# Spectral mixer with a gated MLP: roundings and rests of operands queued apart, two weight loads on GpSimd's queue, 128 spare bytes for 192

## The chip, the cores and the metric

The kernel runs on one core of a Trainium2 chip. The metric is the device time of one execution in microseconds, lower is better. The core has five engines that work through queues of their own and wait for each other by semaphores: TensorE (PE in the profile; its weight loads are PEld), VectorE (DVE), ScalarE (ACT), GpSimd (POOL) and SyncE (SP). In this kernel SyncE only issues DMAs, and GpSimd only DMAs as well, apart from making an identity matrix.

## What is computed

All data is float32: x has 2048 tokens of 512 features.

```python
x = A_x
xn = layernorm(x)
a = einsum("bsd,ed->bse", xn, dft_hid_re)          # 512 x 512
b = einsum("bsd,ed->bse", xn, dft_hid_im)
s = einsum("ts,bse->bte", dft_seq_re, a) - einsum("ts,bse->bte", dft_seq_im, b)   # 2048 x 2048
y = layernorm(xn)
h = gelu(einsum("bsd,df->bsf", y, w1) + b1)        # 512 -> 1792
g = silu(einsum("bsf,fd->bsd", h, w2) + b2)        # 1792 -> 512
return x + s * g
```

## The kernel before

**Two numbers for one.** A float32 product runs on TensorE in the fp32r type. Each operand is split in two: `hi` is the value rounded to fp32r, written by ScalarE (line 64), and `lo` is the rest, `src - hi`, written by VectorE (line 65). A product is three matmuls: hi x hi, hi x lo, lo x hi. So every operand costs one ScalarE instruction and then one VectorE instruction that needs it. `split_into`, `split` and `split_two` issue the two next to each other.

**Seven products for eight.** The larger matrix products are done by Strassen-Winograd steps: sums of quarters of the operands are formed first (`a_sums`, `y_sum`, `w1_sums`), then seven products, then sums of results.

**Stages.** (1) For the first half of the tokens, transposes and the hidden DFT (`dft_mm`, `dft_out`), i = 0 to 7. (2) For the second half the hidden DFT by seven products, `q_product(1)` to `q_product(7)`, in the order 1, 2, 5, 6, 3, 7, 4; each has four column blocks c, and after each block the steps that are listed in the call are queued. (3) The first MLP layer: seven groups j of w1, each with seven products p (`h_product`, line 624), in the order of `h_seq`. Groups 0 and 1 are done for one half of the tokens (tau 1, `ONE`) first, then for the other (tau 0, `ZERO`); groups 2 to 6 for both at once. (4) The second MLP layer (`m_product`). (5) The sequence DFT with the gate and the output. Stages 4 and 5 run their matmuls in `multiply_by` (line 809) and line 1127.

**Order.** The program is scheduled by hand: each engine's queue has its instructions in the order in which the Python code issues them, and an engine whose next instruction waits does nothing else. What stands where in the code is therefore the schedule. Products of stage 2 and 3 take moving or stationary operands called y (from the normalised input, tau 0 and 1, in the versions 11, 21, 22, t1, t2, t3, t4), A (from the DFT weights) and w1.

**Around the change.** `y_centre` and `y_scale` apply mean and scale to the transposed input; `y_sum` forms t1 to t4 in place. `w1_load` (SyncE, line 425) fetches a group's weights into the one buffer of the pool `wr`, so it waits until the rest of the group before has read it; `w1_sums` forms four sums; `w1_split` rounds and rests all seven operands (128 x 1792). In stage 3, product p of a group goes to one of three accumulators (y for 1, 6, 7, 4; z for 5, 3; x for 2). `h_after` copies the accumulator after 1, 5 and 6 on ScalarE (line 640), adds it on VectorE after 2, 3 and 7 (lines 669, 675, 679) with a gelu behind it (line 629), and takes a gelu straight from it after 4. Since 1, 6, 7 and 4 share one accumulator, product 6 waits for the copy after 1, product 7 for the copy after 6, and product 4 for the addition after 7. Product 4 of a group stands in the sequence behind product 5 of the next group. `y_late` lists what is issued just before a product of the groups 0 and 1 in their first half.

**Memory.** The pool `op` (39 tiles of 4,096 bytes a partition) holds operands and guests; behind it lie the constants, among them a tile `spare` that nothing uses (line 105), then `small`, and then the pools that change with the stages (`lpa`, `fp`; later `wr`, `wp` with the w1 operands, `lpm`; later `lp`, `gp`). In each partition the compiled kernel has `op` from byte 16,512, the constants from 176,256, and `wr` and `wp` from 180,416 and 188,608.

Of the kernel before, what the change touches and what calls it, by code (L numbers as in the profile page):

```python
# [8 lines left out]
F32 = mybir.dt.float32  # L9
F32R = mybir.dt.float32r  # L10
BF16 = mybir.dt.bfloat16
I32 = mybir.dt.int32
AF = mybir.ActivationFunctionType
ALU = mybir.AluOpType

P = 128
W = 512
# [5 lines left out]
def fnet_mixer_kernel(ctx: ExitStack, tc: tile.TileContext, x, xT, ct, wt, w1, w2, b1, b2, out):  # L23
    nc = tc.nc
# [11 lines left out]
    consts = ctx.enter_context(tc.tile_pool(name="consts", bufs=1))  # L36
# [9 lines left out]
    def operand(name):  # L46
        return op.tile([P, 2, W], F32R, tag="op", name=name)
# [15 lines left out]
    def split_into(hi, lo, src):  # L63
        nc.scalar.activation(hi, src, AF.Copy)  # L64
        nc.vector.tensor_sub(lo, src, hi.bitcast(F32))  # L65
# [6 lines left out]
    def split_two(src, name):  # L72
        hi, lo = operand(name + "h"), operand(name + "l")
        split_into(hi, lo, src)
        return hi, lo

    def both(row):
        return row[:, None, :].broadcast_to([P, 2, W])

# [22 lines left out]
    sq = consts.tile([P, NC], F32, name="sq")  # L102


    consts.tile([P, 3 * W // 32], F32, name="spare")


    def stats(mv, t, i):
# [101 lines left out]
    room_w = {}  # L210
# [203 lines left out]
    def xt_prepare(b):  # L414
        for k in range(NK // 2):
            xt_centre(b, k)
        for k in range(NK // 2):
            xt_make(b, k)


    w1_raw, w1_op = {}, {}

    def w1_load(j):
        w1_raw[j] = wr.tile([P, 8, 2 * P], F32, tag="w", name=f"w1r{j}")
        nc.sync.dma_start(out=w1_raw[j][:, 4:, :], in_=w1[j])

    def w1_sums(j):
        s1, s2, s3, s4, a11, a12, a22, a21 = (w1_raw[j][:, q, :] for q in range(8))
# [2 lines left out]
        nc.vector.tensor_sub(s2, s1, a11)  # L431
        nc.vector.tensor_sub(s4, a12, s2)

    def w1_split(j):
        hi, lo = (wp.tile([P, 7, 2 * P], F32R, tag="w", name=f"w1{v}{j}") for v in "hl")
        split_into(hi, lo, w1_raw[j][:, :7, :])
        w1_op[j] = (hi, lo)

    y_raw, y_op = {}, {}

    def y_centre(b, k2):
        nc.vector.tensor_add(xtr[b, k2], xtr[b, k2], both(mrow[b]))

    def y_scale(k2, b):
        nc.vector.tensor_mul(xtr[b, k2], xtr[b, k2], both(rrow[b]))
        y_raw[f"{k2 + 1}{b % 2 + 1}", b // 2] = xtr[b, k2]

    def y_split(name, tau):  # L450
        y_op[name, tau] = split_two(y_raw[name, tau], f"y{name}_{tau}")


    def y_sum(dst, tau):
        place, a, b = {"t1": ("11", "12", "11"), "t2": ("t1", "22", "t1"), "t3": ("12", "22", "12"),
                       "t4": ("t2", "21", "t2")}[dst]
        t = y_raw[dst, tau] = y_raw[place, tau]
        nc.vector.tensor_sub(t, y_raw[a, tau], y_raw[b, tau])
# [8 lines left out]
        nc.vector.tensor_sub(a11, a22, a11)  # L467
        nc.vector.tensor_sub(a12, a12, a11)

    def a_split(p):  # L470
        m, k2 = {5: (1, 1), 6: (0, 0), 3: (0, 1), 7: (1, 0)}[p]
        hi, lo = split_two(room_w[m, k2], f"A{p}")
        a_op[p] = [(hi[:, k, :], lo[:, k, :]) for k in range(2)]

    RIGHT = {1: "11", 2: "21", 3: "22", 4: "t4", 5: "t1", 6: "t2", 7: "t3"}
    KEY_Q = {1: "y", 6: "y", 7: "y", 4: "y", 5: "z", 3: "z", 2: "x"}
# [13 lines left out]
    def q_after(p, c):  # L490
        i, j = 2 * NC + c, 3 * NC + c
        f, g = (qq[:, t - HB:t - HB + 1] for t in (i, j))
        nf, ng = (nq[:, t - HB:t - HB + 1] for t in (i, j))
        acc = qx[KEY_Q[p], c]
        if p in (1, 5, 6, 4):
            e = q_place(p, c)
            nc.scalar.activation(e, acc, AF.Copy, scale={1: f, 5: ng, 6: g, 4: nf}[p])
            if p == 4:
                q_out(i, 1, e)
        else:  # L500
            e = q_part[{2: 1, 3: 6, 7: 5}[p], c - c % 2][:, c % 2, :]
            nc.vector.scalar_tensor_tensor(e, acc, {2: f, 3: g, 7: ng}[p], e, op0=ALU.mult, op1=ALU.add)
            q_out(*{2: (i, 0), 3: (j, 0), 7: (j, 1)}[p], e)

    def q_mm(p, c):
        key = KEY_Q[p]
        yh, yl = y_op[RIGHT[p], 1]
        if p in (1, 5, 2):
            qx[key, c] = bank(f"q{key}{c}")
        cols = slice(c * P, (c + 1) * P)  # L510
        terms = [(a[:, k, cols], w) for k in range(2)
                 for a, w in ((yh, a_op[p][k][0]), (yh, a_op[p][k][1]), (yl, a_op[p][k][0]))]
        for n, (a, w) in enumerate(terms):
            nc.tensor.matmul(qx[key, c], a, w, start=p in (1, 5, 2) and n == 0,
                             stop=p in (2, 3, 4) and n == len(terms) - 1, skip_group_check=True)

    def q_product(p, *steps):
        for c in range(NC):
            q_mm(p, c)
            if p in (1, 5, 6, 4):  # L520
                q_after(p, c)
            for do in steps[c:c + 1]:
                for o in do:
                    o()

    for i in range(3, HB):
        if i == 3:
            xt_prepare(1)
            for q in (14, 15):
                act_stats(q)  # L530
            for q in (10, 11):
                stats(mv1, xs[q], q)
            neg_means(2)
            neg_means(0)
        if i == 4:
            second_factors()
        if i == 5:
            a_sums()
            last_factors()
        if i == 6:  # L540
            for k2 in range(2):
                y_centre(2, k2)
            y_scale(0, 2)
            y_split("11", 1)
        if i == 7:
            y_scale(1, 2)
            y_split("21", 1)
            for k2 in range(2):
                y_centre(3, k2)
        dft_mm(i, 0)  # L550
        dft_out(i - 1, 1)
        if i == 4:
            row_st["n"] = nm
            rows_turn("n")
            mrow[2], mrow[3] = row_load("n", 2)
        dft_mm(i, 1)
        dft_out(i, 0)
        if i == 4:
            row_st["R"] = rr[:, HB:3 * HB]
            rows_turn("R")  # L560
            rrow = [None] * 2 + row_load("R", 2, 2)
# [5 lines left out]
    def post(p, *cs):  # L567
        return lambda: [q_after(p, c) for c in cs]

    def then(f, *a):  # L570
        return lambda: f(*a)

    y_scale(0, 3)
    y_sum("t1", 1)
    q_product(1, [then(a_split, 5)], [then(y_split, "t1", 1)], [then(y_scale, 1, 3)], [then(y_sum, "t2", 1)])
    rrow[0:2] = row_load("R", 2)
    centred_load(0)
    q_product(2, [post(2, 0), then(y_split, "t2", 1)], [post(2, 1)], [then(a_split, 6), post(2, 2)], [post(2, 3)])
    q_product(5, [then(y_split, "22", 1)], [then(y_sum, "t3", 1), then(a_split, 3)], [then(y_split, "t3", 1)])
    q_product(6, [then(y_sum, "t4", 1), then(a_split, 7)], [then(y_split, "t4", 1)])  # L580
    early.close()
    wr = early.enter_context(tc.tile_pool(name="wr", bufs=1, reuse_waits="tile"))
    wp = early.enter_context(tc.tile_pool(name="wp", bufs=4, reuse_waits="tile"))
    lp = early.enter_context(tc.tile_pool(name="lpm", bufs=2, reuse_waits="tile"))
    w1_load(0)
    q_product(3, [post(3, 0), then(y_scale, 0, 0)], [post(3, 1), then(y_scale, 0, 1)], [post(3, 2)],
              [post(3, 3), then(w1_sums, 0)])
    q_product(7, [post(7, 0)], [post(7, 1), then(w1_split, 0), then(w1_load, 1)], [post(7, 2)], [post(7, 3)])
    q_product(4, [then(y_split, "11", 0)], [then(y_sum, "t1", 0), then(y_scale, 1, 1)], [then(y_split, "t1", 0)],
              [then(w1_sums, 1)])  # L590

    rows_ps.close()
    yp = ctx.enter_context(tc.tile_pool(name="yp", bufs=4, space=bass.MemoryType.PSUM, reuse_waits="tile"))
# [159 lines left out]
    ONE, ZERO = slice(1, 2), slice(0, 1)  # L753
    h_parts = [(0, ONE), (1, ONE), (0, ZERO), (1, ZERO)] + [(j, TAUS) for j in range(2, NJ)]
    h_seq, last = [], None
    for j, s in h_parts:
# [1 line left out]
        h_seq += [(j, p, s, done) for p in (1, 5)] + ([(last[0], 4, last[1], None)] if last else [])  # L758
        h_seq += [(j, p, s, done) for p in (6, 2, 3, 7)]
        last = j, s  # L760
    y_late = {(0, 1): lambda: (w1_split(1), w1_load(2)),
              (0, 5): lambda: y_sum("t2", 0),
              (0, 6): lambda: y_scale(1, 0),
              (0, 2): lambda: y_split("t2", 0),
              (0, 7): lambda: y_split("21", 0),
              (1, 1): lambda: y_split("22", 0),
              (1, 5): lambda: y_sum("t3", 0),
              (1, 6): lambda: y_split("t3", 0),
              (1, 2): lambda: y_sum("t4", 0),
              (1, 3): lambda: y_split("t4", 0)}  # L770


    m_order = [1, 4, 2, 5, 6, 3, 7]
# [192 lines left out]
            w2_load(1, 1)  # L966

    for j, p, s, done in h_seq:
        if s == ONE and (j, p) in y_late:
            y_late[j, p]()  # L970
        h_product(j, p, s)
        if j == NJ - 1:
            last_chunk(p)
        h_after(j, p, s, done)
        if j == NJ - 1:

            m_ahead("split", {3: 2, 7: 4}.get(p, 0))
            if p == 3:
                m_round(2)
        if stores:  # L980
            store()
        if p == 4 and s.start == 0 and j + 2 < NJ:
            w1_sums(j + 2)
            w1_split(j + 2)
            if j + 3 < NJ:
                w1_load(j + 3)
        if 0 < j < NJ - 1 and s.start == 0 and p in (1, 2, 3):
            extras[j - 1][{1: 0, 2: 1, 3: 2}[p]]()
# [194 lines left out]
```

## Time and profile before

| | us |
|---|---|
| median of three runs | 685.98 (684.87 to 686.95) |
| the profiled execution, whole | 684.43 |
| its span in the profile | 682.4 |
| TensorE busy | 668.3 |
| VectorE busy | 544.2 |
| ScalarE busy | 354.0 |
| GpSimd busy | 49.7 |

Mean granted TensorE clock: 0.996. The span runs from the first to the last instruction that the profiler recorded; the whole execution has 2.03 us around it. Busy times are summed over the instructions of an engine. A line of a timeline gives start and duration in microseconds, engine, line of the code, operation, output and inputs, and in brackets how long the engine had been idle and what released it. The three columns behind the engines in a table by stretches are the granted clock, the mean busy share of the DMA engines, and GB/s.

### The profile page before, as it was taken

Reading aid. Unit: us, or ns where it says so; the run is one execution under the profiler, and the core shown is the slowest. Engines: PE = TensorE matmul, PEld = TensorE weight load, DVE = VectorE, ACT = ScalarE, POOL = GpSimd, SP = SyncE. Lnnn points to the kernel's source line nnn. Section 1 sums busy time; section 2 is a strip of 40 time slices with the busy share of each in tenths; the row PEclk is TensorE's granted clock in tenths of the full one; section 3 lists DMA queues with packets and bytes.
Section 4 is the critical chain, followed back from the end, with each engine's and each line's share of the span. In section 5 each row is a group of like instructions: output and inputs, shape, how many; then the busy total and the mean of one; then the engine's idle time right before and its main releaser. Section 6 shows DMA issues by size and latency. Waiting matters only on the chain.

```text
span 682.4 us, 8159 instructions
## 1 busy us (share of the span) xinstructions
PE 668.3 (98%) x2908; PEld 543.4 (80%) x2908; DVE 544.2 (80%) x592; ACT 354.0 (52%) x395; POOL 49.7 (7%) x82
## 2 busy tenths in 40 slices
PE   8999989999999999999999999999999999999996
PEld 4888867777888888888888888888888888888885
DVE  6979986587887685677997999739977489998985
ACT  4736556544444656565355564437445364646540
POOL 1001000122221010000000100000000001220100
PEclk9999999999999999999999999999999999999999
DMA  8868344398989998578989998425644548996883
GB/s 300 272 246 219 121 137 141 141 329 322 398 303 334 400 416 337 191 267 298 330 303 406 375 341 302 148 67 177 194 155 114 163 110 254 301 252 243 304 263 123
DMA packets 70327, 172.26 MB, mean 252 GB/s; under 512 B 6640, under 2 KB 21008, under 8 KB 70288
## 3 DMA queue, kind: packets, MB, share of 16 engines
q1 hardware_dynamic: 58192, 132.40, 55.5%
q0 software_dynamic: 11744, 38.81, 18.1%
q10 hardware_dynamic: 352, 0.54, 0.2%
q8 instruction: 22, 0.36, 0.2%
q14 instruction: 17, 0.14, 0.1%
HBM read 121.38 MB, written 50.35 MB: 252 GB/s over the span
## 4 chain that ended last, share of the span: by engine, by line
PE 76%; issue 3%; DVE 1%; POOL 1%; DMA 1%; ACT 0%; POOLq 0%
PE pz L809 19%; PE px L809 18%; PE ma L809 11%; PE mb L809 8%; PE hy L624 7%; PE pw L809 5%; PE hz L624 3%; PE hx L624 2%; PE px L1127 2%; PE pw L1127 2%; POOL h_d L632 1%; DMA h_d<-hc 1%; DVE hc L679 0%; DVE hu L675 0%; DVE yt_0l L65 0%
## 5 line engine op out<-in xcount | busy, mean ns | idle before, releaser
L915 DVE TENSOR_TENSOR c<-c,c 128x1024 f32<-128x1024 f32 x32 | 39.2, 1224 | 4.8 <-DMA c<-ct 4.8
L629 ACT ACTIVATE hc<-hc,b_t 128x1024 f32<-128x1024 f32 (+1 forms) x18 | 17.3, 963 | 26.7 <-DVE hc L669 23.2
L65 DVE TENSOR_TENSOR R_b1l<-c,R_b1h 128x1024 fp32r<-128x1024 f32 x16 | 19.5, 1222 | 14.0 <-ACT R_b1h L64 10.7
L809 PE MATMUL pw<-R_s1h,L 128*128 128x512 f32 x96 | 29.7, 389 | 0.0
L64 ACT ACTIVATE R_s3h<-c 128x1024 fp32r<-128x1024 f32 x16 | 17.0, 1062 | 23.9 <-DVE c L915 14.1
L64 ACT ACTIVATE R_b2h<-c 128x1024 fp32r<-128x1024 f32 x16 | 16.9, 1059 | 21.8 <-DVE c L920 17.2
L65 DVE TENSOR_TENSOR R_s2l<-c,R_s2h 128x1024 fp32r<-128x1024 f32 x16 | 19.6, 1224 | 8.6 <-PE pz L809 8.6
L65 DVE TENSOR_TENSOR w1l<-w1r,w1h 128x1792 fp32r<-128x1792 f32 x7 | 14.2, 2026 | 15.2 <-ACT w1h L64 15.2
L64 ACT ACTIVATE R_s2h<-c 128x1024 fp32r<-128x1024 f32 x16 | 17.0, 1061 | 16.7 <-PE px L809 9.3
L65 DVE TENSOR_TENSOR R_s3l<-c,R_s3h 128x1024 fp32r<-128x1024 f32 x16 | 19.6, 1228 | 3.8 <-PE pz L809 3.8
L624 PE MATMUL hy<-yt_1h,w1h 128*128 128x512 f32 x42 | 17.0, 406 | 5.6 <-ACT hc L640 3.9
L64 ACT ACTIVATE R_s1h<-c 128x1024 fp32r<-128x1024 f32 x16 | 16.5, 1053 | 11.6 <-DVE c L926 11.6
L64 ACT ACTIVATE R_b1h<-c 128x1024 fp32r<-128x1024 f32 x16 | 16.7, 1053 | 10.7 <-DMA c<-ct 4.7
L923 POOL DMA_DIRECT2D c<-ct x8 | 7.0, 876 | 201.3 <-issue 147.9
L64 ACT ACTIVATE R_a1h<-c 128x1024 fp32r<-128x1024 f32 x16 | 16.9, 1054 | 8.9 <-PE pz L809 7.2
L809 PEld LDWEIGHTS pw<-R_s1h,L 128*128 128x128 f32 x96 | 18.0, 188 | 3.8
L65 DVE TENSOR_TENSOR R_b2l<-c,R_b2h 128x1024 fp32r<-128x1024 f32 x16 | 19.4, 1220 | 1.5 <-PE px L809 1.5
L65 DVE TENSOR_TENSOR R_a1l<-c,R_a1h 128x1024 fp32r<-128x1024 f32 x16 | 19.6, 1222 | 1.3 <-PE px L809 1.1
L65 DVE TENSOR_TENSOR R_s4l<-c,R_s4h 128x1024 fp32r<-128x1024 f32 x16 | 19.6, 1228 | 0.7 <-PE px L809 0.7
L629 ACT ACTIVATE hu<-hu,b_t 128x1024 f32<-128x1024 f32 (+1 forms) x9 | 8.7, 963 | 21.7 <-DVE hu L675 21.7
L920 DVE TENSOR_TENSOR c<-c,c 128x1024 f32<-128x1024 f32 x16 | 19.6, 1225 | 0.4
L64 ACT ACTIVATE R_s4h<-c 128x1024 fp32r<-128x1024 f32 x16 | 16.8, 1052 | 5.0 <-PE pz L809 4.7
(949 smaller groups left out, 2230.3 us busy)
## 6 DMA issues: line engine op xcount, KB each, us to landing
c<-ct SPq DMA_DIRECT2D x68, 512.0 KB, 6.3
m<-h_d SPq DMA_DIRECT2D x48, 512.0 KB, 6.6
h_d<-ht POOLq DMA_DIRECT2D x21, 512.0 KB, 7.3
s_d<-sa SPq DMA_DIRECT2D x32, 256.0 KB, 3.8
la<-s_d SPq DMA_DIRECT2D x32, 256.0 KB, 6.2
h_d<-hc POOLq DMA_DIRECT2D x13, 512.0 KB, 5.2
x<-x SPq DMA_DIRECT2D x16, 256.0 KB, 5.1
sa<-a_d SPq DMA_DIRECT2D x8, 512.0 KB, 5.2
```

The lines of the kernel that those rows point to most:

```text
L64: nc.scalar.activation(hi, src, AF.Copy)
L65: nc.vector.tensor_sub(lo, src, hi.bitcast(F32))
L624: nc.tensor.matmul(acc[:, tau, :], w[:, W1_AT[p], k * P:(k + 1) * P], r[:, k, :], start=p in (1, 5, 2) and i == 0, stop=p in (2, 3, 4) and ...
L629: nc.scalar.activation(dst, src, AF.Gelu_apprx_tanh, bias=b1_t[:, row:row + 1])
L632: nc.gpsimd.dma_start(out=h_d[p, j], in_=t)
L809: nc.tensor.matmul(acc[k][:, tau, :], a, c[:, tau, :], start=first and i == 0, stop=last and i == len(terms) - 1, skip_group_check=True)
L915: nc.vector.tensor_sub(t, t, raw)
L920: nc.vector.tensor_add(raw, raw, t)
L923: nc.gpsimd.dma_start(out=t, in_=ct[1, 1, n], accum_op=ALU.add)
L1127: nc.tensor.matmul(acc[KEY[name]][k][:, tau, :], a[k], c[:, tau, :], start=False, stop=u == us[-1] and i == 2, skip_group_check=True)
```

## The change

Three things change; the set of arithmetic instructions stays the same.

1. `y_split` and `a_split` are replaced by `y_round`/`a_round` (ScalarE) and `y_rest`/`a_rest` (VectorE), which are issued at places of their own; `w1_split` becomes `w1_round` and `w1_rest`, apart for the groups 0 and 1. The lists of steps of the q products and `y_late` are written anew; the products keep their order among themselves, `row_load("R", 2)` and `centred_load(0)` move ahead of `q_product(1)`, and the opening of the w1 pools with `w1_load(0)` ahead of `q_product(6)`.
2. `w1_load` for the groups 1 and 2 is issued from GpSimd's queue.
3. The tile `spare` has 128 bytes a partition for 192.

```diff
-    consts.tile([P, 3 * W // 32], F32, name="spare")
+    consts.tile([P, W // 16], F32, name="spare")
...
+    def rounded(src, name):
+        hi, lo = operand(name + "h"), operand(name + "l")
+        nc.scalar.activation(hi, src, AF.Copy)
+        return hi, lo
+
+    def rest(hi_lo, src):
+        nc.vector.tensor_sub(hi_lo[1], src, hi_lo[0].bitcast(F32))
...
-        nc.sync.dma_start(out=w1_raw[j][:, 4:, :], in_=w1[j])
+        (nc.gpsimd if j in (1, 2) else nc.sync).dma_start(out=w1_raw[j][:, 4:, :], in_=w1[j])
...
         if i == 6:
-            for k2 in range(2):
-                y_centre(2, k2)
+            for b in (2, 3):
+                for k2 in range(2):
+                    y_centre(b, k2)
+        if i == 7:
             y_scale(0, 2)
-            y_split("11", 1)
-        if i == 7:
+            y_round("11", 1)
             y_scale(1, 2)
-            y_split("21", 1)
-            for k2 in range(2):
-                y_centre(3, k2)
+            y_round("21", 1)
+            y_rest("11", 1)
+            y_rest("21", 1)
...
-    y_scale(0, 3)
-    y_sum("t1", 1)
-    q_product(1, [then(a_split, 5)], [then(y_split, "t1", 1)], [then(y_scale, 1, 3)], [then(y_sum, "t2", 1)])
     rrow[0:2] = row_load("R", 2)
     centred_load(0)
-    q_product(2, [post(2, 0), then(y_split, "t2", 1)], [post(2, 1)], [then(a_split, 6), post(2, 2)], [post(2, 3)])
-    q_product(5, [then(y_split, "22", 1)], [then(y_sum, "t3", 1), then(a_split, 3)], [then(y_split, "t3", 1)])
-    q_product(6, [then(y_sum, "t4", 1), then(a_split, 7)], [then(y_split, "t4", 1)])
+    y_scale(0, 3)
+    a_round(5)
+    y_sum("t1", 1)
+    y_round("t1", 1)
+    a_rest(5)
+    y_rest("t1", 1)
+    q_product(1, [then(y_scale, 1, 3), then(y_round, "22", 1)], [then(y_sum, "t2", 1)],
+              [then(y_round, "t2", 1), then(y_rest, "22", 1)], [then(y_rest, "t2", 1), then(a_round, 6)])
+    q_product(2, [post(2, 0), then(a_rest, 6)], [post(2, 1), then(y_sum, "t3", 1)],
+              [post(2, 2), then(y_round, "t3", 1), then(a_round, 3)], [post(2, 3)])
+    q_product(5, [then(a_rest, 3)], [then(y_rest, "t3", 1), then(y_sum, "t4", 1), then(a_round, 7)],
+              [then(y_round, "t4", 1), then(a_rest, 7)], [then(y_rest, "t4", 1)])
...
     w1_load(0)
-    q_product(3, [post(3, 0), then(y_scale, 0, 0)], [post(3, 1), then(y_scale, 0, 1)], [post(3, 2)],
-              [post(3, 3), then(w1_sums, 0)])
-    q_product(7, [post(7, 0)], [post(7, 1), then(w1_split, 0), then(w1_load, 1)], [post(7, 2)], [post(7, 3)])
-    q_product(4, [then(y_split, "11", 0)], [then(y_sum, "t1", 0), then(y_scale, 1, 1)], [then(y_split, "t1", 0)],
-              [then(w1_sums, 1)])
+    q_product(6, [then(y_scale, 0, 0), then(y_round, "11", 0)], [then(y_scale, 0, 1)],
+              [then(y_rest, "11", 0), then(y_sum, "t1", 0)], [then(y_round, "t1", 0)])
+    q_product(3, [post(3, 0), then(y_rest, "t1", 0)], [post(3, 1), then(w1_sums, 0)], [then(w1_round, 0), post(3, 2)],
+              [post(3, 3)])
+    q_product(7, [post(7, 0)], [post(7, 1), then(w1_rest, 0), then(w1_load, 1)], [post(7, 2)],
+              [post(7, 3), then(y_scale, 1, 1)])
+    q_product(4, [then(y_sum, "t2", 0), then(y_round, "t2", 0)], [then(y_rest, "t2", 0)], [then(w1_sums, 1)],
+              [then(y_scale, 1, 0)])
...
-    y_late = {(0, 1): lambda: (w1_split(1), w1_load(2)),
-              (0, 5): lambda: y_sum("t2", 0),
-              (0, 6): lambda: y_scale(1, 0),
-              (0, 2): lambda: y_split("t2", 0),
-              (0, 7): lambda: y_split("21", 0),
-              (1, 1): lambda: y_split("22", 0),
-              (1, 5): lambda: y_sum("t3", 0),
-              (1, 6): lambda: y_split("t3", 0),
-              (1, 2): lambda: y_sum("t4", 0),
-              (1, 3): lambda: y_split("t4", 0)}
+    y_late = {(0, 5): [then(w1_round, 1)],
+              (0, 6): [then(y_round, "21", 0), then(y_rest, "21", 0), then(w1_rest, 1), then(w1_load, 2)],
+              (0, 2): [then(y_round, "22", 0)],
+              (0, 3): [then(y_rest, "22", 0), then(y_sum, "t3", 0), then(y_round, "t3", 0)],
+              (0, 7): [then(y_rest, "t3", 0), then(y_sum, "t4", 0)],
+              (1, 1): [then(y_round, "t4", 0), then(y_rest, "t4", 0)]}
```

More of the change, by code (lines that the diff above doesn't have):

```diff
@@ L432, in w1_sums, with w1_round, w1_rest @@
         nc.vector.tensor_sub(s4, a12, s2)
+    def w1_round(j):
+        w1_op[j] = [wp.tile([P, 7, 2 * P], F32R, tag="w", name=f"w1{v}{j}") for v in "hl"]
+        nc.scalar.activation(w1_op[j][0], w1_raw[j][:, :7, :], AF.Copy)
+    def w1_rest(j):
+        rest(w1_op[j], w1_raw[j][:, :7, :])
     def w1_split(j):
-        hi, lo = (wp.tile([P, 7, 2 * P], F32R, tag="w", name=f"w1{v}{j}") for v in "hl")
-        split_into(hi, lo, w1_raw[j][:, :7, :])
-        w1_op[j] = (hi, lo)
+        w1_round(j)
+        w1_rest(j)
     y_raw, y_op = {}, {}
@@ L448, in y_scale, with y_round, y_rest @@
         y_raw[f"{k2 + 1}{b % 2 + 1}", b // 2] = xtr[b, k2]
[L450 to L451 removed]
+    def y_round(name, tau):
+        y_op[name, tau] = rounded(y_raw[name, tau], f"y{name}_{tau}")
+    def y_rest(name, tau):
+        rest(y_op[name, tau], y_raw[name, tau])
     def y_sum(dst, tau):
@@ L468, in a_sums, with a_round, a_rest @@
         nc.vector.tensor_sub(a12, a12, a11)
-    def a_split(p):
-        m, k2 = {5: (1, 1), 6: (0, 0), 3: (0, 1), 7: (1, 0)}[p]
-        hi, lo = split_two(room_w[m, k2], f"A{p}")
+    A_ROOM = {5: (1, 1), 6: (0, 0), 3: (0, 1), 7: (1, 0)}
+    a_two = {}
+    def a_round(p):
+        a_two[p] = rounded(room_w[A_ROOM[p]], f"A{p}")
+        hi, lo = a_two[p]
         a_op[p] = [(hi[:, k, :], lo[:, k, :]) for k in range(2)]
+    def a_rest(p):
+        rest(a_two[p], room_w[A_ROOM[p]])
     RIGHT = {1: "11", 2: "21", 3: "22", 4: "t4", 5: "t1", 6: "t2", 7: "t3"}
@@ L968, in fnet_mixer_kernel @@
     for j, p, s, done in h_seq:
-        if s == ONE and (j, p) in y_late:
-            y_late[j, p]()
+        for o in y_late.get((j, p), ()) if s == ONE else ():
+            o()
         h_product(j, p, s)
```

## The prediction

> **What bounds the kernel now.** The page's first and fourth parts come first: how busy each engine is, and what the chain that ended last is made of.
>
> ```profile
> PE 668.3 (98%) x2908; PEld 543.4 (80%) x2908; DVE 544.2 (80%) x592; ACT 354.0 (52%) x395; POOL 49.7 (7%) x82
> PE 76%; issue 3%; DVE 1%; POOL 1%; DMA 1%; ACT 0%; POOLq 0%
> ```
>
> TensorE is busy for 668.3 of 682.4 us, so only two things pay: its idle stretches, and the time from one matmul to the next. The busy times in stretches of 10 us show where it idles (PE, PEld, DVE, ACT, POOL, then the granted clock).
>
> ```profile
> 90.00:100.00 10.00, 6.59 (x29) 5.10 (x28) 8.01 (x9) 5.70 (x8) 0.00 (x0) 0.99 0.50 188
> 100.00:110.00 10.00, 9.85 (x36) 7.55 (x36) 6.85 (x8) 6.25 (x8) 0.00 (x0) 0.84 0.78 262
> 110.00:120.00 10.00, 9.40 (x40) 6.96 (x38) 6.35 (x6) 5.51 (x8) 0.00 (x0) 1.00 0.01 2
> 120.00:130.00 10.00, 8.56 (x37) 6.93 (x38) 4.02 (x7) 5.58 (x9) 0.58 (x1) 1.00 0.08 31
> ```
>
> These are the first products of `h_seq`, around which `y_late` puts the operands. The timeline of TensorE there (start, duration):
>
> ```profile
> 94.93 0.39 PE L624 MATMUL hz<-yt_1h,w1l 128*128 128x512 f32 x1
> 98.73 0.50 PE L624 MATMUL hy<-yt_1h,w1h 128*128 128x512 f32 x1 [3.41 <-ACT hc L640]
> ...
> 99.77 0.61 PE L624 MATMUL hy<-yt_1l,w1h 128*128 128x512 f32 x1
> ...
> 103.16 0.41 PE L624 MATMUL hz<-y_1h,w1h 128*128 128x512 f32 x1
> ...
> 108.55 0.39 PE L624 MATMUL hz<-yt_1h,w1l 128*128 128x512 f32 x1
> 109.09 0.50 PE L624 MATMUL hy<-yt_1h,w1h 128*128 128x512 f32 x1
> ...
> 110.35 0.39 PE L624 MATMUL hy<-yt_1h,w1l 128*128 128x512 f32 x1
> 111.27 0.50 PE L624 MATMUL hy<-yt_1h,w1h 128*128 128x512 f32 x1 [0.53 <-ACT hc L640]
> ...
> 119.54 0.39 PE L624 MATMUL hz<-yt_0h,w1l 128*128 128x512 f32 x1
> 121.44 0.50 PE L624 MATMUL hy<-yt_1h,w1h 128*128 128x512 f32 x1 [1.51 <-DVE hc L679]
> ```
>
> A matmul's step here is 0.233 us. So product 6 of group 0 waits 98.73 - 94.93 - 0.23 = 3.57 us, product 4 of group 0 0.31, product 6 of group 1 0.69, product 4 of group 1 1.67. Eight steps from 99.77 to 103.16 take 3.39 instead of 1.87: 1.52 us go to a lower clock (the 0.84 above) after the long wait. What ends the waits is queue order:
>
> ```profile
> 96.50 1.70 ACT L64 ACTIVATE w1h<-w1r 128x1792 fp32r<-128x1792 f32 x1 [2.19 <-DVE w1r L432]
> 98.10 0.58 ACT L640 ACTIVATE hc<-hy 128x512 f32<-128x512 f32 x1
> ...
> 107.21 1.23 DVE L65 TENSOR_TENSOR y_0l<-xT,y_0h 128x1024 fp32r<-128x1024 f32 x1 [1.74 <-ACT y_0h L64]
> 108.35 0.68 DVE L679 TENSOR_TENSOR hc<-hc,hy 128x512 f32<-128x512 f32 x1
> ```
>
> The copy that product 6 needs stands on ScalarE behind the rounding of group 1's weights, which waits for VectorE's sums; the addition that product 4 needs stands on VectorE behind rests that wait for ScalarE.
>
> **The change part by part.** No instruction is added or dropped except that two loads change queues; the order changes, and 64 bytes of padding go.
>
> The padding: by the addresses of the kernel before, the `op` tiles lie at 16,512 + 4,096n in a partition, a multiple of 128; the w1 operands lie at 188,608 and on, 64 past one. With 64 bytes less, they start at 188,544 and are congruent to the `op` tiles modulo 512. The matmuls of L624 (w1 operands) and of L809 in stretches without a wait:
>
> ```profile
> 163.31:233.57 70.26, 70.26 (x301) 56.66 (x302) 1.00 0.93 340
> ...
> 277.31:372.51 95.20, 95.20 (x421) 78.83 (x421) 1.00 0.81 292
> ```
>
> and, in the groups by shape and on the page, what one takes (mean ns after the comma):
>
> ```profile
> L624 PE MATMUL hx<-y_0h,w1h 128*128 128x512 f32 x6 | 2.4, 396 | 0.0
> ...
> L809 PE MATMUL pw<-R_s1h,L 128*128 128x512 f32 x96 | 29.7, 389 | 0.0
> ```
>
> 70.26/301 = 0.2334 with a w1 operand as the stationary side; 95.20/421 = 0.2261 (0.2267 from the starts) with an `op` tile there. Shapes, types, PSUM pool and moving side are alike, so I put the 6.7 ns to the address. Bounds for one matmul: 0 (another cause) to 6.7 ns saved; I take 6.7, since the only difference I find is the one removed. There are 7 groups x 84 = 588 such matmuls.
>
> The order is counted with these steps (timeline of VectorE, then of ScalarE):
>
> ```profile
> 46.41 1.23 DVE L447 TENSOR_TENSOR xT<-xT,rowR 128x1024 f32<-128x1024 f32 x1 [1.92 <-DMA rowR<-rdR]
> ...
> 81.20 1.40 DVE L502 SCALAR_TENSOR_TENSOR q<-qz,qq,q 128x512 f32<-128x512 f32 x2
> ...
> 94.92 0.42 DVE L429 TENSOR_TENSOR w1r<-w1r 128x256 f32<-128x256 f32 x1
> ...
> 98.23 2.03 DVE L65 TENSOR_TENSOR w1l<-w1r,w1h 128x1792 fp32r<-128x1792 f32 x1 [1.76 <-ACT w1h L64]
> 100.17 1.22 DVE L458 TENSOR_TENSOR xT<-xT,xT 128x1024 f32<-128x1024 f32 x1
> 101.30 1.22 DVE L447 TENSOR_TENSOR xT<-xT,rowR 128x1024 f32<-128x1024 f32 x1
> ...
> 89.07 1.05 ACT L64 ACTIVATE y_0h<-xT 128x1024 fp32r<-128x1024 f32 x1
> 90.02 0.68 ACT L497 ACTIVATE q<-qy,nq 128x512 f32<-128x512 f32 x1
> ```
>
> On VectorE an operand's step is 1.14 us (101.30 - 100.17 = 1.13), a w1 rest 1.94 (2.03 less overlap), the four w1 sums 1.46, a post 0.66, an addition of half an accumulator 0.6; on ScalarE a rounding takes 1.05 (step 0.95), a w1 rounding 1.70, a copy 0.58 (step 0.48). Block 3's two centres move into the 1.92 us that VectorE idled ahead of 46.41, and cost nothing. The rests no longer follow their own rounding at once, which spares most of the 1.1 us waits. Carried through the new order, VectorE starts `a_rest(6)` at 64.4, `y_scale(0, 0)` at 75.3 and `w1_rest(0)` at 87.0. The same count over the old order reaches group 1's sums at 94.5, where the row has 94.92; I add that 0.4: 87.4. TensorE's products 1 to 7 of the q stage find their operands (product 7's last, `a_rest(7)`, ends about 74, needed at 81.5).
>
> From 87.4, on VectorE: posts 89.3 and 90.0, `y_scale(1, 1)` 90.7, `y_sum t2` 91.9 to 93.1; ScalarE's rounding to 94.2; rest t2 94.3; group 1's sums 95.4 to 97.0; `y_scale(1, 0)` to 98.0. ScalarE: w1 rounding 97.0 to 98.7, copy c5, rounding of y21 99.1 to 100.1. VectorE: rest y21 100.2, `w1_rest(1)` 101.3, addition c1 103.25, rest y22 103.85, `y_sum t3` 105.0 to 106.2, addition u2, then a wait for t3's rounding until 107.3, rest t3 107.35, `y_sum t4` 108.5, addition c5 109.6 to 110.3. TensorE: product 6 of group 0 waits about 0.9 for the c1 copy (ScalarE at 95.9, behind t2's rounding and three q copies), so starts at 96.5; product 1 of group 1 waits 0.9 for `w1_rest(1)`; product 4 of group 0 could start at 105.6 and starts at 110.35. **The old 3.57 us wait goes, and a new one of 4.7 us stands at product 4, for VectorE.** Behind that addition wait its gelu, t4's rounding and group 1's c1 copy, so product 6 of group 1 waits as before (0.8 against 0.69). Only one rest stands behind it on VectorE instead of four steps, so the 1.67 us before product 4 of group 1 go.
>
> Sum, from product 4 of group 0 on: +1.25 (110.35 for 109.09), +0.1, -1.67 and its restart of 0.1, and a lower clock again after a wait longer than 3.57, 1.52 less 0.2 that the next wait takes in: +1.3. That is +0.9 for the order. The 588 - 48 = 540 matmuls from there on save 0.0067 each: -3.6. **Together -2.7 to -2.8 us.** The clock's share has bounds 0 and 3.0 (two such stretches).
>
> The loads through GpSimd: group 1's is issued at 89.4 and needed at 95.4, group 2's about 103 and needed after 130.
>
> ```profile
> 131.05 0.53 POOL L632 DMA_DIRECT2D h_d<-ht  x1
> ```
>
> ```profile
> h_d<-ht POOLq DMA_DIRECT2D x9, 512.0 KB, 6.3
> ...
> w1r<-w SPq DMA_DIRECT2D x6, 512.0 KB, 4.1
> xT<-xT POOLq DMA_DIRECT2D x1, 512.0 KB, 7.1
> ```
>
> The first is from the timeline, the others are issues with the median time to landing in 60 to 180 us. The old queue's landing is 4.1 us; GpSimd's for the same size 6.3 and 7.1, both under more traffic or with an addition. I take 5, inside the 6.0 us of slack: nothing; at 7.1 it costs 1.1. SyncE's stores no longer stand behind the wait of that load, nothing on TensorE waits for them. GpSimd has nothing queued behind group 2's load until the h stores at 128. `row_load` and `centred_load` are issued earlier, for operands used at 75: nothing; the `op` slots change hands in another order, which I bound by 1 us either way.
>
> The profiled execution took 684.43 us for a span of 682.4, 1.55 below the median of 685.98. 682.4 - 2.8 = 679.6 of span, 681.7 for such an execution, **683.2** as a median.
>
> **The rivals.** *The address is not the cause.* Then -3.6 goes and +0.9 stays: 686.9. For it speaks that no row shows the same operand at another address. The Trainium skill's SBUF — State Buffer, Specifications (TRN2), gives lines of 16 bytes; 64 and 128 are both multiples, so by that rule nothing changes; the 396 against 389 ns has no place in it.
>
> *VectorE gets through sooner.* If its waits of 2.2 and 0.6 us for ScalarE in the chain above close, product 4 starts near 107.5, 2.8 sooner, the wait is about 2 us, which at 121.44 (1.67) left the clock whole: -2.8 - 2.8 - 1.3 = -6.9; halfway, with the clock kept, -5.4: 680.6. ScalarE's 5.70 of 10 us busy speaks for room; its order, fixed, against.
>
> *The load comes late (slower than before).* Place: group 1's sums. ScalarE's w1 rounding and all copies queue behind them, so each microsecond past 95.4 is one of TensorE. It breaks even at a landing 6.0 + 2.8 = 8.8 us after issue. If descriptors get written only when VectorE pauses, at 95.4 for want of this load, it lands 4.1 later, +4.1: 687.3. Against it: the row at 131.05 issues in 0.53 us while VectorE works. The Trainium skill's SBUF — State Buffer, SBUF: two separate sides, warns that a DMA from GpSimd's queue starves while VectorE runs a 2-port perf-mode op; whether the tensor-tensor steps here count is what that row speaks against.
>
> **How the numbers follow.** Forecast 0.52 (681.7 to 685); address 0.17; sooner 0.18; late load 0.08; the rest, 0.05, is slots. A measurement here tells about 0.3%, 2.06 us, from no change. Faster by that: two thirds of the forecast (0.35), all of "sooner": 0.53. Slower: part of the late load, the address case with a further microsecond, and slots: 0.09. Same: 0.38. The range runs from below 680.6 to the late load's 687.3: 680.0 to 687.3.
>
> **What would show it.** Right: L624 matmuls at 389 ns and a step of 0.2267; TensorE's longest wait at product 4 of group 0, released by the addition of L679's kind, near 110; the clock down in 110 to 120; no wait at 121. Wrong: 396 ns (address); no wait over 2 us between 92 and 125 (VectorE sooner); group 1's sums released by the load (late).

## The result and the profile after

| | before | after |
|---|---|---|
| median of seven runs each, taken together (us) | 685.05 (684.82 to 686.95) | 681.35 (679.95 to 683.11) |
| the profiled execution, whole | 684.43 | 681.11 |
| its span | 682.4 | 679.3 |
| TensorE busy | 668.3 | 664.6 |

The ratio is 0.9941, with a 95% interval of 0.9924 to 0.9958: faster by 3.7 us in the medians and 3.1 us in the spans. In the code after, the matmuls of stage 3 are line 657 (624 before), `multiply_by` 838 (809), the additions of accumulators 702, 708 and 712 (669, 675, 679), their copies on ScalarE 673 (640), roundings 79, rests 83.

The busy times on the page of the kernel after, then its stretches of 10 us (PE, PEld, DVE, ACT, POOL, granted clock, DMA share, GB/s):

```profile
PE 664.6 (98%) x2908; PEld 543.2 (80%) x2908; DVE 544.2 (80%) x592; ACT 354.3 (52%) x395; POOL 50.6 (7%) x84
```

```profile
90.00:100.00 10.00, 8.24 (x37) 6.50 (x36) 6.63 (x10) 6.82 (x10) 0.00 (x0) 1.00 0.91 302
100.00:110.00 10.00, 5.68 (x26) 4.39 (x25) 9.20 (x9) 4.93 (x7) 0.56 (x1) 1.00 0.19 65
110.00:120.00 10.00, 10.00 (x38) 8.06 (x38) 3.29 (x4) 5.88 (x10) 0.00 (x0) 0.83 0.01 2
120.00:130.00 10.00, 10.00 (x46) 8.28 (x45) 3.23 (x5) 5.05 (x8) 0.75 (x2) 1.00 0.13 52
```

The hole in TensorE has moved from the first stretch into the second, where VectorE is busy 9.20 of 10 us, and the lower clock has moved behind it. TensorE's timeline there:

```profile
94.27 0.50 PE L657 MATMUL hy<-y_1h,w1h 128*128 128x512 f32 x1 [1.76 <-ACT q L520]
...
95.77 0.39 PE L657 MATMUL hz<-yt_1h,w1h 128*128 128x512 f32 x1
...
97.13 0.39 PE L657 MATMUL hy<-yt_1h,w1h 128*128 128x512 f32 x1
...
105.07 0.39 PE L657 MATMUL hz<-yt_1h,w1l 128*128 128x512 f32 x1
109.78 0.70 PE L657 MATMUL hy<-yt_1h,w1h 128*128 128x512 f32 x1 [4.32 <-DVE hc L712]
...
112.42 0.63 PE L657 MATMUL hy<-yt_1h,w1h 128*128 128x512 f32 x1
113.27 0.42 PE L657 MATMUL hy<-yt_1h,w1l 128*128 128x512 f32 x1
...
121.05 0.39 PE L657 MATMUL hy<-yt_1h,w1h 128*128 128x512 f32 x1
```

Four readings. From 95.77 to 97.13 there are six steps: 0.2267 us each. Product 6 of group 0 (97.13) starts without a wait. Product 4 of group 0 starts at 109.78, 109.78 - 105.07 - 0.23 = 4.48 us late. The eight steps behind it, to 113.27, take 3.49 instead of 1.81, so 1.68 us go to the clock and to the restart (the first step behind a wait is some 0.1 us longer). Product 6 of group 1 (112.42) and product 4 of group 1 (121.05) don't wait.

VectorE's and then ScalarE's timeline show what stood ahead:

```profile
106.77 1.23 DVE L83 TENSOR_TENSOR yt_0l<-xT,yt_0h 128x1024 fp32r<-128x1024 f32 x1 [0.53 <-ACT yt_0h L79]
107.91 1.22 DVE L475 TENSOR_TENSOR xT<-xT,xT 128x1024 f32<-128x1024 f32 x1
109.04 0.68 DVE L712 TENSOR_TENSOR hc<-hc,hy 128x512 f32<-128x512 f32 x1
```

```profile
92.59 1.06 ACT L79 ACTIVATE yt_0h<-xT 128x1024 fp32r<-128x1024 f32 x1 [3.43 <-DVE xT L475]
93.55 1.83 ACT L520 ACTIVATE q<-qy,nq 128x512 f32<-128x512 f32 x3
```

The addition for product 4 stands behind the rest of t3 and the sum t4, neither of which anything needs soon. The 1.76 us ahead of 94.27 are the same kind of wait on ScalarE: the last copies of the q stage stand behind t2's rounding, and group 0's first accumulator needs what they free.

Up to product 4 of group 1, the start went from 121.44 to 121.05, only 0.39 sooner: +0.69 at product 4 of group 0 (109.09 to 109.78), -0.69 and -1.77 for the waits of group 1's products 6 and 4 that are gone (1.67 and its restart), +1.68 for the clock, and 42 steps of 0.0067. The other 2.7 us come behind it, where the order of work is the same: some 500 matmuls, 0.0067 shorter each, are 3.3. A part of that is given back at one place, read in the timelines of VectorE and TensorE, of the kernel before and then after:

```profile
158.13 0.69 DVE L704 TENSOR_TENSOR sa<-sa,sa 128x512 f32<-128x512 f32 x1 [2.74 <-DMA sa<-b_d]
...
163.31 0.50 PE L624 MATMUL hy<-yt_0h,w1h 128*128 128x512 f32 x1 [0.51 <-DVE hc L679]
```

```profile
157.66 0.69 DVE L737 TENSOR_TENSOR sa<-sa,sa 128x512 f32<-128x512 f32 x1 [2.95 <-DMA sa<-b_d]
...
162.84 0.50 PE L657 MATMUL hy<-yt_0h,w1h 128*128 128x512 f32 x1 [1.18 <-DVE hc L712]
```

VectorE waits there for a load, and the addition that TensorE needs is queued behind it; TensorE arrives sooner and waits 0.67 us longer.

### The profile page after: what moved, and what is told of

It reads as the page before. It is cut to its first block, busy times and chain, and to the rows that moved or that the text cites. A ratio compares the mean times of both kernels' runs of the same rounds, so it can differ in the third digit from the quotient of the medians.

```text
span 679.3 us, 8185 instructions
## 1 busy us (share of the span) xinstructions
PE 664.6 (98%) x2908; PEld 543.2 (80%) x2908; DVE 544.2 (80%) x592; ACT 354.3 (52%) x395; POOL 50.6 (7%) x84
## 4 chain that ended last, share of the span: by engine, by line
PE 84%; DVE 5%; issue 5%; DMA 2%; ACT 2%; POOL 1%; SPq 0%; POOLq 0%; DVEq 0%; ACTq 0%
PE pz L838 19%; PE px L838 18%; PE ma L838 11%; PE mb L838 8%; PE hy L657 8%; PE pd L338 6%; PE pw L838 5%; PE hz L657 3%; PE hx L657 2%; PE px L1156 2%; PE pw L1156 2%; POOL h_d L665 1%; DMA rw<-wt 1%; DVE xT L475 1%; DVE q L525 1%
## 5 line engine op out<-in xcount | busy, mean ns | idle before, releaser
L64 ACT ACTIVATE w2h<-w 128x1024 fp32r<-128x1024 f32 (+1 forms) x14 | 13.2, 946 | 12.8 <-DVE w L770 3.9
```

## The experiments

The theory: the padding brings about 3 us through the step of stage 3, the order nearly nothing, because the wait it takes away comes back at product 4 with its lower clock, and the loads nothing. The rivals: the address is not the cause of the shorter step; the order carries the gain; the load's queue does. Ratios are against the kernel before, run beside.

### The padding alone, and the order alone

The first kernel is the one before with the one line of the padding changed; the second is the one after with that line put back.

```diff
-    consts.tile([P, 3 * W // 32], F32, name="spare")
+    consts.tile([P, W // 16], F32, name="spare")
```

> The kernel before with 128 spare bytes and nothing else. If the address of the w1 operands sets the step of their matmuls: 389 ns for 396, a step of 0.2267 for 0.2333 us, and the four waits of before stay and grow by what TensorE then arrives earlier (about 0.1 to 0.3 each): 3.0 to 3.8 us less than before. If the address is not the cause: step 0.2333, 0.0.

> The changed kernel with 192 spare bytes, so the new order and the two loads alone. If the step hangs on the address: 0.2333 again, the wait of 4.3 us at product 4 of group 0 stays (a little shorter), and the time is 0 to 1.5 us above before. If the order is what gains: 2 us or more below before.

Padding alone: 681.89 against 684.93, ratio 0.9966 (0.9953 to 0.998). Order and loads without the padding: 684.17 against 684.93, ratio 0.9987 (0.9978 to 0.9997). The stretch 180 to 230 of stage 3, counting the h matmuls alone (PE, PEld, clock, DMA share, GB/s), in the kernel before, after, with the padding alone and with the order (and the loads) alone:

```profile
180.00:230.00 50.00, 50.00 (x216) 40.30 (x215) 1.00 0.94 338
```

```profile
180.00:230.00 50.00, 50.00 (x222) 41.42 (x221) 1.00 0.96 346
```

```profile
180.00:230.00 50.00, 50.00 (x223) 41.39 (x222) 1.00 0.95 343
```

```profile
180.00:230.00 50.00, 50.00 (x216) 40.30 (x215) 1.00 0.93 336
```

The count in 50 us follows the padding and nothing else. So the padding is the larger part, 3.0 us alone and 684.17 - 681.35 = 2.8 on top of the order. I had expected the order alone to be 0 to 1.5 us slower, which it isn't: it gains 0.8 us in the medians, 0.2 to 1.5 by the interval of its ratio. With the padding alone the gain is not whole either, as the waits of the kernel before and of the padding alone show (what waits and for what: us in total, times, longest):

```profile
PE hy L624 <- ACT hc L640: 3.9, 2, 3.4
PE hy L624 <- DVE hc L679: 2.0, 2, 1.5
```

```profile
PE hy L624 <- ACT hc L640: 4.0, 2, 3.5
PE hy L624 <- DVE hc L679: 3.4, 4, 1.7
```

A TensorE that is done sooner waits 1.4 us longer for the same additions on VectorE.

### The same padding in other sizes, and the other operand moved

If the address is the cause, what about it? In the kernel after, the `op` tiles and the w1 operands both lie at 128 modulo 512. One address modulo 512 stands for all tiles of a side: an `op` tile has 4,096 bytes and a w1 tile 7,168, both multiples of 512, and so are the parts that a matmul takes. Five kernels change the size of `spare`, or put a small pool ahead of `op`, or both; the sizes in bytes are in the table below, and the edit shown is that of the kernel with 64 and 64.

```diff
+    pre = ctx.enter_context(tc.tile_pool(name="pre", bufs=1))
+    pre.tile([P, W // 32], F32, name="pre")
     op = ctx.enter_context(tc.tile_pool(name="op", bufs=39))
...
-    consts.tile([P, W // 16], F32, name="spare")
+    consts.tile([P, W // 32], F32, name="spare")
```

> The changed kernel without the spare tile: w1 operands at 188,416, a multiple of 128 (and 128 off the op tiles modulo 256 and 512). If a multiple of 128 is what counts: step 0.2267. If the w1 operands must lie congruent to the op tiles modulo 256 or 512: 0.2333.

> The changed kernel with 64 spare bytes: w1 operands at 188,480, 64 past a multiple of 128, the op tiles unmoved. If a multiple of 128 counts: step 0.2333 in stage 3 as with 192 bytes. If 192 bytes were bad for another reason: 0.2267.

> The changed kernel with 64 bytes ahead of the op pool and 64 fewer behind the constants: op tiles at 64 past a multiple of 128, w1 operands at one as in the changed kernel. If the stationary side's address sets the step: 0.2267 in stage 3 and 0.2333 in the stages whose stationary side is an op tile (about 2,300 matmuls, 15 us longer). If the moving side's: 0.2333 in all. If only the two sides' difference: 0.2333 in stage 3, 0.2267 elsewhere.

> The kernel after with 64 unused bytes ahead of the op pool and its own 128 spare bytes: the op tiles lie at 192 modulo 512 and the w1 operands at 192 as well, both 64 past a multiple of 128, and equal to each other. Theory (what counts is that the two operands of a matmul have the same address modulo 512): the step of the L657 matmuls is 0.2267 us, x220 or more of them in 180 to 230 us, mean 389 ns. Rival (a multiple of 128 of at least one side counts): the step stays near 0.2289 or goes to 0.233, 392 to 396 ns.

> The kernel after with 384 spare bytes: the op tiles lie at 128 modulo 512, the w1 operands at 384, so 256 apart. Theory with a period of 512 bytes: the step of the L657 matmuls is near 0.233 us (394 to 397 ns, x216 in 180 to 230 us), and the time about 3 us above the kernel after. Theory with a period of 256 or less: 0.2267 us (389 ns, x221).

The same stretch of the h matmuls, in this order (no spare; 64 spare; 64 ahead of `op` and 64 spare; 64 ahead and 128 spare; 384 spare):

```profile
180.00:230.00 50.00, 50.00 (x217) 40.54 (x216) 1.00 0.93 341
```

```profile
180.00:230.00 50.00, 50.00 (x216) 40.52 (x215) 1.00 0.90 322
```

```profile
180.00:230.00 50.00, 50.00 (x220) 41.05 (x219) 1.00 0.95 343
```

```profile
180.00:230.00 50.00, 50.00 (x222) 41.39 (x221) 1.00 0.96 349
```

```profile
180.00:230.00 50.00, 50.00 (x222) 41.39 (x221) 1.00 0.96 346
```

| ahead of op, spare | op and w1, modulo 512 | h matmuls in 50 us | one run (us) |
|---|---|---|---|
| 0, 192 (before, and order alone) | 128, 192 | 216 | |
| 0, 64 | 128, 64 | 216 | 686.2 |
| 0, 0 | 128, 0 | 217 | 683.17 |
| 64, 64 | 192, 128 | 220 | 682.87 |
| 0, 128 (after) | 128, 128 | 222 | |
| 64, 128 | 192, 192 | 222 | 684.22 |
| 0, 384 | 128, 384 | 222 | 681.71 |

Two rules fall. "A multiple of 128 is fast" falls with no spare: 0 is a multiple of 128, and the step stays long. "Equal modulo 512" falls with 384 spare, where the operands are 256 apart and the step is short. What fits all seven is that the step is shortest where moving and stationary side have the same address modulo 256, and that it doesn't matter which address that is. The kernels of the other experiments fit too: away from the waits the step is 0.2267 us in all eight with equal addresses, and 0.2289 to 0.2333 in the five others. The largest group of matmuls with `op` tiles on both sides (96 in line 838, 809 before) stays at 389 ns in every one. So the padding does it. That it acts through the two operands of the matmul is the likeliest reading and not shown by itself, since every pool behind `spare` moves with the w1 operands.

How much is lost with unequal addresses is open. Where `op` and the w1 operands both moved (64 and 64), I had expected 0.2267 or 0.2333 and got 0.2289. And in the one run with 64 spare, where w1 lies 64 below `op` as well, the step changes on the way, as TensorE's timeline shows:

```profile
153.70 0.39 PE L657 MATMUL hy<-yt_0h,w1l 128*128 128x512 f32 x1
...
161.26 0.40 PE L657 MATMUL hz<-yt_1h,w1l 128*128 128x512 f32 x1
163.57 0.50 PE L657 MATMUL hy<-yt_0h,w1h 128*128 128x512 f32 x1 [1.92 <-DVE hc L712]
...
168.48 0.40 PE L657 MATMUL hy<-yt_0h,w1l 128*128 128x512 f32 x1
...
171.98 0.40 PE L657 MATMUL hx<-y_0h,w1l 128*128 128x512 f32 x1
```

Up to 161.26, 33 steps take 0.229 each, as with 64 and 64; from 168.48 on, fifteen take 0.2333. Between the two lie a wait and a stretch at the lower clock. So its 216 holds for the stretch 180 to 230 alone, and the layout doesn't settle how long the longer step is.

The single times order the kernels less well than the counts do, since the lower clock comes in at different places. The kernel with 64 ahead and 128 spare has the short step and 684.22 us. Its TensorE, in stretches of 2 us at the start:

```profile
8.00:10.00 2.00, 0.26 (x1) 0.26 (x2) 0.28 (x1) 0.94 (x2) 0.00 (x0) 1.00 0.73 280
10.00:12.00 2.00, 2.00 (x7) 1.57 (x7) 1.93 (x5) 1.69 (x4) 0.00 (x0) 0.67 0.81 285
12.00:14.00 2.00, 2.00 (x6) 1.51 (x6) 2.00 (x4) 0.83 (x2) 0.00 (x0) 0.50 0.96 291
```

In this execution it idled in the first stage, waiting for the first weights, and then ran at the lower clock. Its stage 3 started at 96.81 for 94.27 in the kernel after. The 686.2 us of the run with 64 spare have 1.6 us of lower clock in them too, behind the wait at 163.57. A count in a stretch without waits has none of this.

### The loads on SyncE's queue again

```diff
-        (nc.gpsimd if j in (1, 2) else nc.sync).dma_start(out=w1_raw[j][:, 4:, :], in_=w1[j])
+        nc.sync.dma_start(out=w1_raw[j][:, 4:, :], in_=w1[j])
```

> The changed kernel with the w1 loads of groups 1 and 2 on SyncE's queue. If GpSimd's queue matters for the load itself: group 1's lands at another time; it has some 1.5 us of slack before the sums, so the time stays within 0.5 us. What moves is SyncE's stores, which stand behind the load's wait for the rest of group 0; nothing on TensorE waits for them in the trace: 0. If the freed SyncE queue is worth something: 1 us or more above the changed kernel.

682.51 against 684.74, ratio 0.9965 (0.9952 to 0.9978), which overlaps the 0.9924 to 0.9958 of the kernel after. The median is 1.2 us above that of the kernel after, where I had expected at most 0.5 and named 1 us or more as the sign of the rival. The intervals overlap only a little, but the lower clock, different from one execution to the next, lies over the difference: the mean granted clock is 0.993 in eight of the twelve executions here, and in two of the seven of the kernel after. A version without that clock is needed, below.

### Operands that nobody needs yet, put behind the additions

If VectorE's queue is the wait at product 4, then the rest of t3 and the sum t4 put behind that addition take some 3 us from it, and a wait that short may leave the clock whole.

```diff
-              (0, 7): [then(y_rest, "t3", 0), then(y_sum, "t4", 0)],
-              (1, 1): [then(y_round, "t4", 0), then(y_rest, "t4", 0)]}
+              (1, 1): [then(y_rest, "t3", 0), then(y_sum, "t4", 0)],
+              (1, 6): [then(y_round, "t4", 0), then(y_rest, "t4", 0)]}
```

> The changed kernel with two VectorE steps (rest of t3, sum t4) moved from ahead of the addition after product 7 of group 0 to behind it. If the wait at product 4 is VectorE's queue: the addition 2.3 us sooner (two steps of 1.14), the wait near 2 us, the clock stays whole (1.7 us not lost): 3 to 4 us below the changed kernel, less what a later wait takes back. If the wait has another cause: no change.

678.09 against 684.93, ratio 0.9917 (0.9892 to 0.9942). TensorE's and VectorE's timelines and the stretch behind:

```profile
106.81 0.50 PE L657 MATMUL hy<-yt_1h,w1h 128*128 128x512 f32 x1 [1.43 <-DVE hc L712]
```

```profile
106.07 0.68 DVE L712 TENSOR_TENSOR hc<-hc,hy 128x512 f32<-128x512 f32 x1
```

```profile
110.00:120.00 10.00, 10.00 (x46) 8.28 (x45) 3.20 (x4) 5.18 (x9) 0.00 (x0) 1.00 0.01 2
```

The addition comes 2.97 us sooner (109.04 before the move), the product too, and the lower clock is gone: 46 matmuls in the stretch for 38. VectorE's queue was the cause. This is the fastest of the six executions; two others, of 682.5 and 680.7 us, had a mean granted clock of 0.994 and 0.996 where the rest have 0.998 to 1.000, so the lower clock seems to be gone in most of them, not in all. What stays is the wait for the q copies, behind t2's rounding. So the next kernel puts the rests of all five late operands (t2, 21, 22, t3, t4) behind group 0's additions, and t2's rounding out of the way of those copies.

```diff
-    q_product(4, [then(y_sum, "t2", 0), then(y_round, "t2", 0)], [then(y_rest, "t2", 0)], [then(w1_sums, 1)],
-              [then(y_scale, 1, 0)])
+    q_product(4, [then(y_sum, "t2", 0)], [], [then(w1_sums, 1)], [then(y_scale, 1, 0)])
...
-              (0, 6): [then(y_round, "21", 0), then(y_rest, "21", 0), then(w1_rest, 1), then(w1_load, 2)],
-              (0, 2): [then(y_round, "22", 0)],
-              (0, 3): [then(y_rest, "22", 0), then(y_sum, "t3", 0), then(y_round, "t3", 0)],
-              (0, 7): [then(y_rest, "t3", 0), then(y_sum, "t4", 0)],
-              (1, 1): [then(y_round, "t4", 0), then(y_rest, "t4", 0)]}
+              (0, 6): [then(w1_rest, 1), then(w1_load, 2)],
+              (0, 2): [then(y_round, "t2", 0)],
+              (0, 3): [then(y_round, "21", 0)],
+              (1, 1): [then(y_rest, "t2", 0), then(y_rest, "21", 0)],
+              (1, 5): [then(y_round, "22", 0), then(y_rest, "22", 0), then(y_sum, "t3", 0)],
+              (1, 6): [then(y_round, "t3", 0), then(y_rest, "t3", 0)],
+              (1, 3): [then(y_sum, "t4", 0)],
+              (1, 4): [then(y_round, "t4", 0), then(y_rest, "t4", 0)]}
```

> The changed kernel with all of t2, 21, 22, t3 and t4 behind the additions of group 0, and the rounding of t2 out of the q copies' way. If TensorE only waits for queue order here: no wait over 0.5 us from 92 to 125, clock whole, about 8 us below the changed kernel by the count of waits, less what the DMA-bound stretch at 140 to 165 takes back (there TensorE already waited 0.7 us more than before when it came 1.1 us sooner), so 5 to 8 below it. If the work only moves: less than 3.

**672.57 against 684.93, ratio 0.9831 (0.9815 to 0.9847)**, faster than both kernels. Its stretches:

```profile
90.00:100.00 10.00, 10.00 (x46) 8.29 (x45) 7.95 (x10) 7.23 (x10) 0.56 (x1) 1.00 0.90 313
100.00:110.00 10.00, 10.00 (x46) 8.26 (x45) 7.69 (x8) 7.22 (x11) 0.00 (x0) 1.00 0.16 55
110.00:120.00 10.00, 10.00 (x46) 8.29 (x45) 5.00 (x8) 6.09 (x10) 0.54 (x1) 1.00 0.05 20
```

TensorE has no hole left there. Against the kernel after, 8.8 us go, more than the 5 to 8 that I had expected; the two waits and the clock read above make 1.76 + 4.48 + 1.68 = 7.9 of them. The VectorE column shows that it is less busy from 100 to 110 (7.69 for 9.20), and busier later: no work is gone, it stands where nobody queues behind it.

This version has no lower clock in stage 3, so the loads were compared in it, with the same edit as above:

> The version with all of the late operands behind group 0's additions (e4_defer_all), with the w1 loads of the groups 1 and 2 on SyncE's queue again. TensorE has no wait over 1 us in that version, and the lower clock does not come in, so the loads can be compared without it. Theory (the queue of the loads is worth nothing): 672.6, ratio to the kernel before 0.983, the same within 0.002. Rival (GpSimd's queue spares a late load or takes one out of the way of SyncE's other issues): 673.5 to 676, and the sums of group 1 wait for a DMA on VectorE.

673.66 against 685.06, ratio 0.9838 (0.981 to 0.9866): no difference that this tells from 0.9831. The time lies 1.1 us above 672.57, though, within the 673.5 to 676 that I had given to the rival. On VectorE, group 1's first sum does wait for the load, here with GpSimd's queue and then with SyncE's:

```profile
93.26 0.43 DVE L437 TENSOR_TENSOR w1r<-w1r 128x256 f32<-128x256 f32 x1 [1.16 <-DMA w1r<-w]
```

```profile
92.49 0.42 DVE L437 TENSOR_TENSOR w1r<-w1r 128x256 f32<-128x256 f32 x1 [0.27 <-DMA w1r<-w]
```

GpSimd's comes 0.77 us later, and TensorE is busy 10.00 of 10 us in either. So the longer wait for the load is on GpSimd's side, not on SyncE's as my rival had it, and costs TensorE nothing. A part of the difference of the profiled executions comes later: at 154 us TensorE waits 1.29 us with SyncE's queue and 0.82 with GpSimd's, for an addition that stands behind VectorE's wait for a load on SyncE's queue (3.08 and 2.60 us). Whether the w1 loads on that queue bring this about is not shown. So the loads are worth about a microsecond in the medians (1.2 and 1.1 us), in favour of GpSimd's queue if at all; that they are worth nothing is not shown.

## Why the prediction was right, step by step

**The padding, 540 steps of 0.0067 us: right in mechanism and in the size of the step.** Forecast 389 ns and 0.2267, measured both. The 3.6 us came out as 3.0 alone and 2.8 on top of the order, since waits further on take some of it in: 0.67 us at 162.84 in the kernel after, 1.4 in the first groups with the padding alone. The prediction costed no such thing. Its working, a congruence modulo 512, was narrower than what the runs showed: modulo 256 is enough. The rival that the address is not the cause is refuted, as far as the runs can tell: one line that moves addresses and nothing else makes 216 into 223.

**The order, VectorE's chain: right.** `w1_rest(0)` was carried to 87.0 and raised to 87.4 by the difference of one row; it started at 86.77. The same shift runs through to the end: the addition was put at 109.6 and stood at 109.04. The 0.4 that I added was most of the error, so +1.25 at product 4 was in truth +0.69.

**The wait at product 4: right** (4.7 forecast, 4.48 measured, the releaser and the lower clock in 110 to 120 as foretold). **The two waits of 0.9 us were in the wrong place.** I had counted that the q copies stand behind t2's rounding, but let TensorE go on and wait at product 6. Group 0's first accumulator needs the room of those copies, so it waited 1.76 us at 94.27, and product 6 and `w1_rest(1)` were then in time. That the sum, 1.8, comes out the same is chance, and neither enters the forecast: product 4 waited for VectorE's addition either way.

**Group 1's product 6: wrong, +0.1 for a true -0.69.** The lower clock just ahead stretched the products before it, so the copy was there in time. The clock itself took 1.68, of which the forecast of 1.3 had left out 0.2 for exactly this overlap: too little. **Product 4 of group 1: right**, no wait.

So the order was forecast at +0.9 us and stood at about -0.1 in this execution (0.69 - 0.69 - 1.77 + 1.68); alone it gained 0.2 to 1.5 us. That is the weakest term: its sign was wrong. The sum of -2.8 was only 0.3 short of the span's -3.1, and that is luck in part: the order came out 1.0 better than forecast, and the later waits, which had no term, took back 0.6 to 0.8 of the padding's 3.6. In the medians the forecast of 683.2 was 1.9 too high; 0.9 of that is only that the kernel before had a median of 685.05 beside it, not 685.98.

**The loads: forecast nothing, and right but for the microsecond that the runs leave open.** From issue to landing group 1's took 4.6 us, I took 5. The rival that descriptors are late while VectorE works is not what this case shows; the timeline of GpSimd after has the issue at 89.09, in the middle of VectorE's work:

```profile
89.09 0.57 POOL L433 DMA_DIRECT2D w1r<-w  x1 [30.06 <-DVE w1l L83]
```

**VectorE sooner:** 0.57 us of it came true, not the 2.8 that leaves the clock whole. With the two operands deferred it happened just as that rival had it, 2.97 us sooner and the clock whole.

## What to carry to other kernels

In a queue that is written by hand, put a step where its result is needed, not where its input is ready: taking work off the critical path moved a wait here from ScalarE to VectorE, and only putting early-issued operands behind the additions that TensorE waits for brought the 8.8 us. Where two groups of matmuls of one shape have different steps, compare the addresses of their operands with each other, and try one small padding. Count what a long wait costs with the lower clock that follows it, and expect the next wait to swallow some of a gain upstream.

## What the runs showed of the hardware

**Two operands' addresses, against each other.** With moving and stationary side equal modulo 256 a step takes 0.2267 us, otherwise 0.2289 to 0.2333 (seven layouts above, same matmuls). The mechanism is open: the runs vary addresses only, and only these seven, and one layout had two steps in one execution. The Trainium skill's TensorE: Matmul & The Clock Gate, Step-by-step: what each phase is for, has two independent read ports, so that loading the next weights takes nothing from the running matmul; by that no layout should differ from another. The measurement decides: 216 against 222 matmuls in 50 us.

**The lower clock's length is not the wait's.** After nearly the same wait at product 4, the order alone lost more than the kernel after. TensorE's timeline of the order alone:

```profile
110.19 0.79 PE L657 MATMUL hy<-yt_1h,w1h 128*128 128x512 f32 x1 [4.06 <-DVE hc L712]
110.78 0.63 PE L657 MATMUL hy<-yt_1l,w1h 128*128 128x512 f32 x1
...
115.90 0.59 PE L657 MATMUL hx<-y_1l,w1h 128*128 128x512 f32 x1
116.33 0.39 PE L657 MATMUL hx<-y_1h,w1l 128*128 128x512 f32 x1
```

Here 14 steps take 6.14 us instead of 3.27, a loss of 2.87; in the kernel after 8 steps lost 1.68. From 110.78 to 115.90 twelve steps take 0.427 each. The granted clock was 0.50 in these stretches of the kernel after, of the order alone and of the kernel with 64 spare, and 1.00 on either side of each:

```profile
109.91:113.32 3.41, 3.41 (x9) 2.64 (x10) 1.23 (x1) 3.15 (x5) 0.00 (x0) 0.50 0.00 0
```

```profile
109.49:116.32 6.83, 6.13 (x14) 4.78 (x15) 1.87 (x3) 3.88 (x6) 0.00 (x0) 0.50 0.00 0
```

```profile
164.88:168.28 3.40, 3.40 (x10) 2.63 (x9) 3.37 (x5) 1.86 (x3) 2.12 (x4) 0.50 0.74 208
```

The lower clock lasts 3.4 us or twice that, and doesn't begin where TensorE begins again: 0.13 us behind it, 0.70 ahead of it and 1.3 behind it in these three (109.78, 110.19, 163.57). In ten of the thirteen traces a wait of 3.4 us or more in stage 3 brought it. In four of them it begins ahead of TensorE's next matmul and lasts 6.8 us, in the other six behind it and lasts 3.4. That goes with losses of some 1.7 or up to 2.9 us behind like waits. The Trainium skill's TensorE: Matmul & The Clock Gate, What's actually happening, has a free-running window of 3.4 us that decides, which agrees with these lengths and with a loss that depends on where the wait falls; its step at the lower clock, given under Wait — 56ns, not 53.3ns?, is 426.7 ns, as here. Waits of up to 1.8 us in stage 3 (idle time in brackets) were followed by a whole clock. The wait of 1.92 us at 163.57 in the kernel with 64 spare was not, and neither was one of 2.2 us in the first stage of another kernel (the stretches from 8 to 14 us above). In the 3.4 us ahead of each such drop TensorE was idle for at least 1.9. So a wait well under 3.4 us can bring the lower clock, and where the limit lies stays open.
